# The convolution's running sum in two PSUM banks instead of the gate's SBUF tile, with another order of all instructions

## The chip, the cores and the metric

One core of a Trainium2 chip runs the whole program. The metric is the device time of one execution in microseconds (us), the median of several runs. The engines are TensorE (PE, with its weight loads shown apart as PEld), VectorE (DVE), ScalarE (ACT), GpSimd (POOL) and SyncE (SP), which issues the transfers. PSUM has eight banks of 512 numbers per partition here; PE writes its results there, and DVE and ACT read and write there too. POOL works on SBUF alone in this kernel.

## What is computed

Eight batches, eight heads, 576 positions, 64 numbers per head. Attention with a causal mask and a decay, then a gated two-layer map in which the gate is a convolution over five positions:

```
scores = q @ k.T / sqrt(64) + (cum[i] - cum[j])      # causal; cum = cumsum(log f)
x      = softmax(scores) @ v                          # (8, 576, 512)
gate   = sigmoid(sum over t of conv_w[t] * xp[:, t:t+576, :])   # xp: x with four zeros in front
out    = (gate * (x @ w_val)) @ w_out
```

## The kernel before

Work goes by pairs of heads: 32 pairs, four to a batch, so that two heads of 64 fill 128 partitions. For each pair the steps are these (the short names are the classes by which the kernel's plan knows them, and the lines are those of the kernel before):

- **TH, TL** (L374 and the helper at L260): the loaded q and k (`Xr`) are split into a high part `Xh` and a rest `Xl`; copies go to ACT, DVE or POOL, the subtraction to DVE or POOL.
- **S**: score matmuls into PSUM (L245, the helper of all matmuls).
- **sel** (L469 on DVE, L467 on POOL, L302 for the short last block): the causal mask is put into the loaded decay row `dm` or `dl`.
- **red** (L458, DVE): adds the decay, scales, and finds the row's bound `negm`; it reads PSUM and SBUF, and writes back into PSUM.
- **SX** (L462, ACT): the exponential, from PSUM to SBUF (`P`, `Pl`).
- **PT** (L503, L527, PE): transposes of the result into PSUM; **PE** (L260) copies them to SBUF (`pt`, `pl`), on ACT or DVE.
- **PV** (PE), **X** (L577, DVE): times v, times the inverse row sum, which has come back through DRAM (`rzd`); the result is `x32`, here called x.
- **xh, xl** (L260, L584): x split into two parts for the next matmul.
- **conv** (L265, L267, L619): five passes over x. The first multiplies x by one weight column into the pair's gate tile in SBUF, on ACT, DVE or POOL; the other four are scalar_tensor_tensor instructions, gate = x * weight + gate, on DVE. A POOL form was allowed for the first four pairs.
- **sig** (L590, ACT): a tanh of the gate tile in place.

After four pairs a batch's gated map follows: **Mv** (PE, x times w_val), **H** (L651, DVE, gate times that), **hh, hl** (L260, L665), **Mo** (PE, times w_out), **O** (L692, L694) and the store.

No scheduler works at run time. A table of digits, three or more for each instruction group, gives one order for the whole program: the group's number, its engine, and the PSUM banks that it takes. Every engine runs its share of this list in that order and waits on semaphores where data or a bank is not ready. A bank taken again waits for all users of what it held. `Plan.order` reads the table; the costs and priorities given to `plan.add` were for the search that made the table, and nothing reads them when the kernel is built.

Of the kernel before, what the change touches and what calls it, by code (L numbers as in the profile page):

```python
# [11 lines left out]
ALU = mybir.AluOpType  # L12
# [4 lines left out]
P = 128  # L17
D = 64
S = 576
# [9 lines left out]
NPT = 4  # L29
# [17 lines left out]
0010930z40240740430K40630q000u30a30V40C20B10D22640b30e20x30r30E20520f10d20F10s30g10h20c328001230G20i20H20I20j40J20M10P20N20Q10O22900R20S20T14040U22R42  # L47
a00X12b21442d22j0452c15b40t20-22e14242f20_12x0100Y22m22g12s062k22n12o22h22l12t00Z22p13-42z11024442y12D0421122i1340012u21212q22F22r11722v11320p052E12A0
233b21f41613722V045672w24642B13522C13925d41923811822G021a12W03a11b23c12X02H11c22Q12I42-21e33613i012K42Y22_15941d22Z13k054c35h21h13222O43023312M41k23d0
33114841i21j21l11q43x0675541m23u0023z12T41n23e03w15741p33y13l23j23v10o053f24a31o13A0160y34m0503B13o23C13p23m14b012763g13q21s13h23n34d24x034f24e10v34h2  # L50
7044g10m014i24k24j14B0214n24l10n074o25j34q24D13D061t24p14s23O013E14t24C11v23H44v23N13r23F44u14w17445i067254y27d34r11w11u23L44z17e33J45m27f14E0037245k2
5n11B45o24F17844H0475r24G13Q003s24J15l14A25p25s14K061x24I15t0354L13R27i35q14M44U25u35I0041z17g34O45v25K15E063P25f45J15x27643S11y27h001425F25z34S45w13T
34Q45A25G15C27j28b45y14V063U37l25B15D17n27m13V25L0537k15H25O0177o21A35P14X005N17q25Q14W27t37r13W27p15R067s0234Y27c35S15_13X20w35V47D008q15T43Y25M17H06
78d44_17w28r37E262054Z15Z47u27F14-25X460041D18j45028o17a47y27J18f41E20l001G27x16n079m47z28p37v17B29s47C16f006327A19q46121H17K0258h47G26415127N0439u47I
16k016527M15227O17Q057R16l05326617U46g01F27-17S45416729o46c057P16827L16d03t16926o03Z16a28s023647Y46e28t36b18n36h27W49B11I281006i18u29z16j27_058v18w29A
36p28x16m28026q18O018y38229C38z28518D0058B28A18S037ax48E28316v068F26r38T18P26w08U18H2aD48Q11J26s076x28J31M48I19E38M21K19D061238628N18K28C11L2az46t08G1
872aB4aM18Y0459w49F28L1aN38-1aF49H28Z18V0059G16u26D048X19J29K2aK31O19O0579M28W19P29I16A06cB48R29S2aP36y11X49Z009y39Q29N11R21P26E09L19-29U36z39T18_029X
29_19V29029149R1842991934a70011Q21S1a10238l4aL2a81cF49Y16B0a911T2954a31882cO1974aO01703cJ4a211U2cP29W1cH4cQ19a05cD4aQ21W3aS2aR19c02a021Z16C2aU3cR3aT1a
# [107 lines left out]
def tile_decay_attention_gated_mlp(  # L166
# [89 lines left out]
    def any_(cls, durs, prio, fn, reads=(), writes=(), **kw):  # L256
        return plan.add(cls, durs, prio, lambda e: fn(engine[e]), reads, writes, **kw)
# [566 lines left out]
```

## Time and profile before

| what | value |
|---|---|
| median of three runs | 530.08 us (527.26 to 532.85) |
| the profiled execution | 531.49 us |
| its span in the trace | 529.8 us |
| PE busy | 487.0 us (92%) |
| weight loads busy | 414.6 us (78%) |
| DVE busy | 468.6 us (88%) |
| ACT busy | 351.4 us (66%) |
| POOL busy | 159.8 us (30%) |
| mean granted TensorE clock | 0.987 |

Busy time is the time in which at least one instruction of the engine was under way. Instructions of one engine overlap a little at their ends, so the durations of single instructions add up to more than the busy time. The span is shorter than the execution's time by 1.7 us, which lie around it.

### The profile page before, as it was taken

To read this page: it belongs to the slowest core of one execution; us is meant where nothing else is said; L and a number is where in the kernel's file an instruction comes from. 1 tells how busy PE (TensorE), PEld (TensorE's weight loads), DVE (VectorE), ACT (ScalarE), POOL (GpSimd) and SP (SyncE) were. 2 spreads that over 40 slices of the span, in tenths; PEclk is the share of its full clock that TensorE was granted. 3 is DMA by queue.
4 is the path that set the end of the run, shared out by engine and by line. 5 is a ranking of instruction groups with operands and counts; after the bars stand their busy time and mean duration, and the time that the engine had idled before them with its cause. 6 is when DMAs were issued, how large, how long until landed. Compare 5 with 4: busy or idle time off the path is not lost.

```text
span 529.8 us, 13876 instructions
## 1 busy us (share of the span) xinstructions
PE 487.0 (92%) x5136; PEld 414.6 (78%) x5136; DVE 468.6 (88%) x1214; ACT 351.4 (66%) x963; POOL 159.8 (30%) x190
## 2 busy tenths in 40 slices
PE   5878989899999989999797999999999989999997
PEld 3656778777899777888696878887778878898985
DVE  6988999999998899999986998999998989989871
ACT  4978989889767664766665676777866647584020
POOL 4132625452234432222423251321312343012210
PEclk9998999899999999999998999999999999999999
DMA  6774465755555356445444437454554555521022
GB/s 205 241 247 113 124 212 151 235 159 177 157 173 172 113 170 174 131 147 173 145 128 127 147 115 251 128 163 133 144 171 142 151 141 176 180 64 37 11 81 99
DMA packets 35012, 79.57 MB, mean 150 GB/s; under 512 B 5056, under 2 KB 5312, under 8 KB 34944
## 3 DMA queue, kind: packets, MB, share of 16 engines
q1 hardware_dynamic: 34864, 78.54, 48.7%
q8 instruction: 40, 0.66, 0.5%
q14 instruction: 28, 0.23, 0.1%
q10 hardware_dynamic: 80, 0.15, 0.1%
HBM read 68.93 MB, written 9.73 MB: 148 GB/s over the span
## 4 chain that ended last, share of the span: by engine, by line
PE 44%; DVE 26%; DMA 12%; ACT 9%; issue 5%; SPq 3%; DVEq 0%; ACTq 0%
PE banks L245 38%; DVE banks L458 8%; DVE gate L619 5%; PE banks L503 4%; DMA x<-rzd 4%; DMA Xr<-in_x_dram 3%; ACT P L462 3%; SPq L271 3%; DVE dm L469 2%; ACT pt L260 2%; DMA rzd<-pl 1%; DVE negm L458 1%; PE banks L527 1%; DVE x L577 1%; ACT Pl L462 1%
## 5 line engine op out<-in xcount | busy, mean ns | idle before, releaser
L462 ACT ACTIVATE P<-banks,negm 128x128 f32<-128x128 f32 (+3 forms) x256 | 135.0, 535 | 63.8 <-DVE negm L458 60.3
L458 DVE CUSTOM_DVE_ANT_0 banks<-banks,dm 128x512 f32<-128x512 f32 (+1 forms) x240 | 115.4, 505 | 15.3 <-ACT pt L260 4.4
L619 DVE SCALAR_TENSOR_TENSOR gate<-x,cw,gate 128x576 f32<-128x576 f32 x128 | 117.6, 927 | 1.4 <-ACT gate L265 0.4
L245 PE MATMUL banks<-xh,wall 128*128 128x288 f32 x512 | 114.5, 304 | 1.2 <-DVE pt L260 0.7
L260 ACT COPY pt<-banks 128x512 f32<-128x512 f32 (+1 forms) x194 | 98.6, 538 | 24.8 <-PE banks L503 21.5
L245 PE MATMUL banks<-pt,vt 128*64 128x128 f32 (+1 forms) x1280 | 95.0, 300 | 1.3 <-DVE pt L260 0.6
L245 PE MATMUL banks<-wall,hh 128*128 128x512 f32 x288 | 91.7, 399 | 2.7 <-ACT P L462 1.6
L245 PEld LDWEIGHTS banks<-xh,wall 128*128 128x128 f32 x512 | 85.7, 189 | 5.8 <-DVE pt L260 0.9
L245 PEld LDWEIGHTS banks<-pt,vt 128*64 128x64 f32 x1280 | 76.2, 138 | 11.0 <-issue 1.8
L245 PE MATMUL banks<-xl,wall 128*128 128x288 f32 x256 | 75.9, 297 | 0.0
L503 PE MATMUL banks<-ident,P 64*128 64x64 f32 x1280 | 59.9, 230 | 16.6 <-ACT P L462 9.2
L503 PEld LDWEIGHTS banks<-ident,P 64*128 64x128 f32 x1280 | 50.2, 141 | 31.8 <-ACT P L462 15.7
L467 POOL TENSOR_SCALAR_AFFINE_SELECT dm<-dm 128x256 f32<-128x256 f32 x51 | 24.4, 481 | 126.7 <-DVE negm L458 48.5
L245 PEld LDWEIGHTS banks<-wall,hh 128*128 128x128 f32 x288 | 51.5, 188 | 13.9 <-ACT P L462 2.4
L374 POOL TENSOR_TENSOR Xl<-Xr,Xh 128x576 fp32r<-128x576 f32 (+1 forms) x30 | 46.1, 1538 | 49.9 <-ACT Xh L260 49.6
L245 PE MATMUL banks<-Xh 64*128 64x512 f32 (+2 forms) x224 | 52.9, 384 | 6.3 <-ACT Pl L462 3.5
L245 PE MATMUL banks<-wall,hl 128*128 128x512 f32 x144 | 56.3, 391 | 0.0
L462 ACT ACTIVATION_READ_ACCUMULATOR P<-banks,negm 128x1 f32 x256 | 53.2, 208 | 0.0
L245 PEld LDWEIGHTS banks<-xl,wall 128*128 128x128 f32 x256 | 48.5, 189 | 0.3
L245 PE MATMUL banks<-Xh,Xl 64*128 64x512 f32 (+2 forms) x224 | 46.6, 333 | 0.0
L245 PE MATMUL banks<-Xl,Xh 64*128 64x512 f32 (+2 forms) x224 | 46.5, 333 | 0.0
L665 POOL TENSOR_TENSOR hl<-h,hh 128x64 fp32r<-128x64 f32 (+2 forms) x22 | 23.5, 1072 | 70.1 <-DVE hh L260 38.8
(100 smaller groups left out, 761.4 us busy)
## 6 DMA issues: line engine op xcount, KB each, us to landing
Xr<-in_x_dram SPq DMA_DIRECT2D x32, 608.0 KB
dm<-decd SPq DMA_DIRECT2D x60, 256.0 KB
vt<-in_v_dram SPq DMA_DIRECT2D x32, 320.0 KB
x<-rzd SPq DMA_DIRECT2D x64, 144.0 KB
out_dram<-ot SPq DMA_DIRECT2D x36, 256.0 KB
dl<-decd SPq DMA_DIRECT2D x60, 144.0 KB
ot<-in_w_val_dram SPq DMA_DIRECT2D x2, 512.0 KB
wu<-in_w_val_dram SPq DMA_DIRECT2D x2, 512.0 KB
```

The source lines that it names most:

```text
L245: nc.tensor.matmul(out, lhsT=lhsT, rhs=rhs, start=start, stop=stop)
L260: (eng.copy if eng is nc.scalar else eng.tensor_copy)(out=out, in_=in_)
L271: lambda e: (nc.sync if e == "SP" else nc.scalar).dma_start(out=out, in_=in_), reads, writes, **kw)
L374: eng.tensor_tensor(out=Xl[r][:, a:e], in0=Xr[r][:, a:e], in1=Xh[r][:, a:e].bitcast(F32), op=ALU.subtract)
L458: nc.vector.tensor_tensor_reduce(out=sl, in0=sl, in1=add, op0=ALU.add, op1=ALU.min, scale=-0.125, scalar=3.0e38, accum_out=negm[r][:, col])
L462: nc.scalar.activation(out=dst[:, o:o + ext], in_=bank(key)[:, c0:c0 + ext], func=AF.Exp, bias=negm[r][:, col], scale=-1.0, accum_out=zs[r ...
L467: eng.affine_select(out=t, in_=t, pattern=[[0, 2], [-1, P]], base=0, channel_multiplier=1, compare_op=ALU.is_ge, fill=-BIG)
L469: eng.tensor_tensor(out=t, in0=t, in1=tri4[:, None, :].to_broadcast([P, 2, P]), op=ALU.add)
L503: nc.tensor.transpose(out=bank(key[a])[:, c:c + D], in_=Pt[ms[h]][sl, BOFF[b] + P * j:BOFF[b] + P * j + P], identity=ident[sl, sl])
L527: nc.tensor.transpose(out=t[0:m, 512 * h + D * j:512 * h + D * j + D], in_=Pl[r][sl, P * j:P * j + m], identity=ident[sl, sl])
L619: eng.scalar_tensor_tensor(out=gt, in0=src, scalar=wt_, in1=gt, op0=ALU.mult, op1=ALU.add)
L665: eng.tensor_tensor(out=hl[jj][:, y:y + x1 - x0], in0=h32[:, x0:x1], in1=hh[jj][:, y:y + x1 - x0].bitcast(F32), op=ALU.subtract)
```

## The change

The sum of the convolution gets two PSUM banks of its own, `acc`, for each pair. The first pass writes there, on DVE or ACT and no longer on POOL; the next three read and write there; the fifth pass reads the banks and writes the gate tile in SBUF. The POOL form of the later passes is gone. Some costs for the search are other numbers, and so is a group label (`mode`) of the transposes; neither reaches the program. The table is new as a whole: the order on every engine, which engine does the work that may go to several, and the banks.

```
-0010930z40240740430K40630q000u30a30V40C20B10D22640b30e20x30r30E20520f10d20F10s30g10h20c328001230G20i20H20I20j40J20M10P20N20Q10O22900R20S20T14040U22R42
+0010930240z40740b30K40s30V40r30C20B10520630a30e20E20D20F10f10G20430H20I20y30J20m000x30h20u30c30d328012340t32T40i20j40N20M12R40P20O20Q10g12900R20S20T10
...
-            pe("PT", 0.0622 * 2 * nt, p, go, [("ident",), *(("P", m, b) for m in ms for b in blocks)], key, cols=256 * nt, mode=1)
+            pe("PT", 0.0622 * 2 * nt, p, go, [("ident",), *(("P", m, b) for m in ms for b in blocks)], key, cols=256 * nt, mode=4)
...
+        acc = new(("acc", i), 2)
         for n, t in enumerate(reversed(range(KC))):
-            early = i < NPT and n > 0
-
-            def cv(eng, t=t, first=n == 0):
+
+            def cv(eng, t=t, n=n):
                 src, wt_ = xr[:, t:t + S], cw[:, t, g:g + 1]
-                if first:
-                    times(eng, gt, src, wt_)
-                elif eng is nc.gpsimd:
-                    times(eng, h32, src, wt_)
-                    eng.tensor_tensor(out=gt, in0=gt, in1=h32, op=ALU.add)
+                sums = bank(acc)[:, 0:S]
+                if n == 0:
+                    times(eng, sums, src, wt_)
                 else:
-                    eng.scalar_tensor_tensor(out=gt, in0=src, scalar=wt_, in1=gt, op0=ALU.mult, op1=ALU.add)
-            any_("conv", {"DVE": 0.76, **({"POOL": 2.2} if early else {})} if n else {"POOL": 0.73, "DVE": 0.45, "ACT": 0.67}, p + 0.1 + 0.02 * n, cv,
-                 [*xk, ("xpad", rx), ("cw",), *([gk] if n else [])], [gk, *(kh32 if early else [])])
+                    eng.scalar_tensor_tensor(out=gt if n == KC - 1 else sums, in0=src, scalar=wt_, in1=sums, op0=ALU.mult, op1=ALU.add)
+            any_("cv", {"DVE": 0.68} if n else {"DVE": 0.68, "ACT": 0.64}, p + 0.1 + 0.02 * n, cv,
+                 [*xk, ("xpad", rx), ("cw",), acc], [gk] if n == KC - 1 else [acc])
```

Lines of the changed kernel stand one to four lower than before (L619 is L615, L458 is L457, L374 is L373).

DVE, where the four later passes of the tenth pair stand (x_94 is its x, gate_110 its gate tile, dm and dl decay rows of later pairs, ISA the red instruction and the read of its result, h_112 of a gated map). In the kernel before, the first pass, one further pass, and the next one ten rows on:

```order
L267 TENSOR_SCALAR gate_110<-x_94,cw 128x576
L619 SCALAR_TENSOR_TENSOR gate_110<-x_94,cw,gate_110 128x576
L458 ISA banks,negm_90<-banks,dm_69 128x512
L458 ISA negm_90 128x1
L458 ISA banks,negm_90<-banks,dm_69 128x512
L458 ISA negm_90 128x1
L577 TENSOR_TENSOR x_95<-banks,x_95 128x192
L477 TENSOR_SCALAR Pl_83<-zs_93 128x9
L478 RECIPROCAL Pl_83<-Pl_83 128x9
L584 TENSOR_TENSOR xl_106<-x_96,xh_100 128x576
L469 TENSOR_TENSOR dm_69<-dm_69,tri_66 128x2x128
L619 SCALAR_TENSOR_TENSOR gate_110<-x_94,cw,gate_110 128x576
```

And in the changed kernel, all four passes of the same pair:

```order
L615 SCALAR_TENSOR_TENSOR banks<-x_94,cw,banks 128x576
L647 SCALAR_TENSOR_TENSOR h_112<-gate_111,banks 128x288
L615 SCALAR_TENSOR_TENSOR banks<-x_94,cw,banks 128x576 x2
L457 ISA banks,negm_91<-banks,dm_70 128x128
L457 ISA negm_91 128x1
L457 ISA banks,negm_91<-banks,dm_70 128x128
L457 ISA negm_91 128x1
L647 SCALAR_TENSOR_TENSOR h_112<-gate_111,banks 128x288
L615 SCALAR_TENSOR_TENSOR gate_110<-x_94,cw,banks 128x576
```

The passes now stand close together, since two banks are held from the first to the last of them; over all pairs DVE begins 4 to 14 groups of work from the first of them to the last, and PE 2 to 9. The second operand is a bank and no longer the gate tile, and the pair's first pass is on ACT.

POOL, from the low part of the tenth pair's x (xl_105) on; Xl_78 is the low part of q and k of the twelfth pair, Xl_77 of the thirteenth. In the kernel before:

```order
L584 TENSOR_TENSOR xl_105<-x_95,xh_99 128x576
L467 AFFINE_SELECT dm_70<-dm_70 128x2x128
L467 AFFINE_SELECT dm_69<-dm_69 128x2x128 x2
L374 TENSOR_TENSOR Xl_78<-Xr_74,Xh_76 128x640
L467 AFFINE_SELECT dm_70<-dm_70 128x2x128 x2
L374 TENSOR_TENSOR Xl_77<-Xr_73,Xh_75 128x576
```

And in the changed kernel:

```order
L583 TENSOR_TENSOR xl_105<-x_95,xh_99 128x576
L466 AFFINE_SELECT dm_69<-dm_69 128x2x128
L301 TENSOR_TENSOR dl_72<-dl_72,tri 128x64
L373 TENSOR_TENSOR Xl_78<-Xr_74,Xh_76 128x640
L373 TENSOR_TENSOR Xl_78<-Xr_74,Xh_76 128x576
```

Both halves of the twelfth pair's Xl are on POOL now, one behind the other, where DVE had the second half.

What the two tables give to each engine, where the numbers differ most:

| work | DVE before | DVE after | other engine before | after |
|---|---|---|---|---|
| conv, passes two to five | 128 | 128 | - | - |
| conv, first pass | 11 | 12 | ACT 12, POOL 9 | ACT 20, POOL 0 |
| mask of dm, 128x256 | 69 | 39 | POOL 51 | POOL 81 |
| mask of dl, 128x64 | 19 | 9 | POOL 11 | POOL 21 |
| Xl, 128x640 | 16 | 5 | POOL 12 | POOL 23 |
| xl, 128x576 | 16 | 9 | POOL 16 | POOL 23 |
| hl, 128x576 | 10 | 6 | POOL 6 | POOL 10 |
| copy of pt, 128x512 | 15 | 37 | ACT 145 | ACT 123 |

On PE the kinds and numbers of all matmuls are the same; only their order and banks differ. The transfers are the same in number and size.

## Rows read from the trace of the kernel before

**Rows 1.** Page, part 1: busy us (share of the span) and instructions of each engine

```profile
PE 487.0 (92%) x5136; PEld 414.6 (78%) x5136; DVE 468.6 (88%) x1214; ACT 351.4 (66%) x963; POOL 159.8 (30%) x190
```

**Rows 2.** Stretches: length, busy of PE, PEld, DVE, ACT, POOL, granted clock, DMA, GB/s

```profile
20.00:480.00 460.00, 428.16 (x4722) 365.70 (x4724) 421.24 (x1110) 329.06 (x919) 145.16 (x160) 0.99 0.52 156
...
0.00:20.00 20.00, 12.60 (x84) 8.21 (x84) 14.88 (x44) 12.61 (x28) 6.40 (x24) 1.00 0.74 245
...
260.00:280.00 20.00, 16.34 (x186) 15.29 (x186) 16.58 (x48) 12.93 (x39) 3.54 (x5) 0.91 0.56 166
280.00:300.00 20.00, 17.18 (x182) 15.87 (x182) 15.27 (x39) 12.20 (x35) 6.31 (x8) 0.91 0.46 134
...
500.00:520.00 20.00, 20.00 (x112) 17.68 (x111) 12.37 (x29) 3.03 (x5) 1.70 (x2) 1.00 0.16 60
```

**Rows 3.** Page, part 4: the chain that ended last, shares of the span by engine

```profile
PE 44%; DVE 26%; DMA 12%; ACT 9%; issue 5%; SPq 3%; DVEq 0%; ACTq 0%
```

**Rows 4.** All waits, longest first: who waited for whom, us, times, longest

```profile
ACT P L462 <- DVE negm L458: 60.3, 52, 3.5
...
PE banks L503 <- ACT P L462: 9.2, 8, 3.0
...
PE banks L245 <- DMA Xr<-in_x_dram: 3.0, 1, 3.0
```

**Rows 5.** DVE by form: count | busy us, mean ns | idle before, releasers

```profile
L619 DVE SCALAR_TENSOR_TENSOR gate<-x,cw,gate 128x576 f32<-128x576 f32 x128 | 117.6, 927 | 1.4 <-ACT gate L265 0.4 <-POOL gate L267 0.4
L469 DVE TENSOR_TENSOR dm<-dm,tri 128x256 f32<-128x256 f32 x69 | 34.8, 507 | 0.9
L651 DVE SCALAR_TENSOR_TENSOR h<-gate,banks 128x288 f32<-128x288 f32 x64 | 27.4, 446 | 4.9 <-PE banks L245 2.4 <-ACT gate L590 1.5
L374 DVE TENSOR_TENSOR Xl<-Xr,Xh 128x640 fp32r<-128x640 f32 x16 | 14.6, 912 | 0.2 <-ACT Xh L260 0.2
L584 DVE TENSOR_TENSOR xl<-x,xh 128x576 fp32r<-128x576 f32 x16 | 12.2, 761 | 0.1
L260 DVE COPY pt<-banks 128x512 f32<-128x512 f32 x15 | 10.1, 681 | 0.8 <-ACT pl L260 0.6 <-PE banks L503 0.2
L665 DVE TENSOR_TENSOR hl<-h,hh 128x576 fp32r<-128x576 f32 x10 | 8.7, 874 | 0.4 <-ACT hh L260 0.4
L267 DVE TENSOR_SCALAR gate<-x,cw 128x576 f32<-128x576 f32 x11 | 7.1, 641 | 0.1
L302 DVE TENSOR_TENSOR dl<-dl,tri 128x64 f32<-128x64 f32 x19 | 5.7, 297 | 0.1
```

**Rows 6.** Lines L619 and L458 (width 576): duration ns min/median/max, first and last start

```profile
L619 DVE SCALAR_TENSOR_TENSOR gate<-x,cw,gate x128: 757/812/2051, 33.9 to 512.2; 128x576 f32<-128x576 f32 x128
...
L458 DVE CUSTOM_DVE_ANT_0 banks<-banks,dl x30: 750/766/799, 45.1 to 476.6; 128x576 f32<-128x576 f32 x30
```

**Rows 7.** Chain in order of time: start us, us, what

```profile
33.87 0.83 DVE gate L619
34.72 2.05 DVE gate L619
```

**Rows 8.** Timeline of POOL at the same place: start us, us, what

```profile
34.75 1.41 POOL L584 TENSOR_TENSOR xl<-x,xh 128x576 fp32r<-128x576 f32 x1 [2.08 <-ACT xh L260]
```

**Rows 9.** ACT and POOL by form, as in rows 5

```profile
L260 ACT COPY pt<-banks 128x512 f32<-128x512 f32 x145 | 82.7, 592 | 18.5 <-PE banks L503 15.4 <-PE banks L527 2.5
L265 ACT ACTIVATE gate<-x,cw 128x576 f32<-128x576 f32 x12 | 9.4, 781 | 2.0 <-DVE x L577 2.0
...
L584 POOL TENSOR_TENSOR xl<-x,xh 128x576 fp32r<-128x576 f32 x16 | 26.4, 1648 | 20.9 <-ACT xh L260 12.6 <-DVE xh L260 8.3
L467 POOL TENSOR_SCALAR_AFFINE_SELECT dm<-dm 128x256 f32<-128x256 f32 x51 | 24.4, 481 | 126.7 <-DVE negm L458 48.5 <-DMA dm<-decd 46.7 <-DVE Pl L477 15.0
L374 POOL TENSOR_TENSOR Xl<-Xr,Xh 128x640 fp32r<-128x640 f32 x12 | 19.3, 1609 | 16.6 <-ACT Xh L260 16.4
L267 POOL TENSOR_SCALAR gate<-x,cw 128x576 f32<-128x576 f32 x9 | 8.0, 891 | 11.8 <-DVE x L577 11.7
```

More of the change, by code (lines that the diff above doesn't have):

```diff
@@ L28 @@
 NXR = 3
-NPT = 4
 R0 = 16
@@ new lines @@
+U32j0562b22d21442c10Y24642a00X12k22642q22e12o20p010-20q072l10Z22s002p12m20_12h22r12t01023-42n12f22i12D0651122g12x0722E21332F12u22A0342y1340562C22v11f4
+1222z14042w22B11722G003921613b22V042732H23522Q12I41921822K41a12W05b43723c11b23a12X02-21d12M43611c23d002O43222_11e32Y24443313i053023811q41i21h14243k063
+111k25741j21l15942Z11m23x0725d43l25543e03y13j23z11n23o143A0363f21p30n073C13p20o023g13u0764c33B13q21s14b001233m13r23w13s23v11o14d24x064f24e13h24m0454g1
+4h35j34i24B0107044a34k24j14C24n34D14q24l13D014o23O003N13E24s33H44p10v34t24v24u13F44y24w15i012344844r11t24z11u23L47f11v24E0675m23J41w13Q055k27245n11B41
@@ new lines @@
+x24F14A25l14H0261y24J25o34I14G15h35r24K010w37d35p25t0675s14L25u34U13R24O43P27g35I0455q17445x25E005v25K17843U225y15z34M41z10l057e35F25f45J13V27645G15C2
+1A35w13W27h045103t14S45A23X25D17i38f45B13n34V077l21D14Q43Y23S18b47m17j25O0635P15H27k15Q27n35R057c25L0231E25S17q25T44X045N17o25V47r11F28d47p11G27s0038h
+44W27t35M13T34Y25_17H0717w24Z17u25Z460064_247J15X47y34-37B29m45027C17D017I19q47z25127x17a48o36f077v17E28j47A162035227F19u48q27G27K0126128r36326n007L15
+326416c038t37M18p26k041H165266117Q051I26d07R17-16727S49z16g07U46829A37N0656h26l07O16e27P13Z16927W48s067356i11J27Y46a25419o46j36o01K18w29s48u28l48x1810
@@ new lines @@
+11L36m21M48v16p26q18y28S0628B27_078T18z28U16r26b18E38D0248028C18n38229y38O068F2ax49E385108H29B38316s058628J38A16t09C38P28I18M26v038Q1872aB48438N18K26w
+0aF46u28G1882aD48L19D045671O19w46x2892aM1aK3az48Y0329F29Z008-19H29G18Z29J39I18V0249-2aN39O0359K29_19M2cB48W18R26D008X29P39N1aL39L18_019S29Q2a104790199
+29T19346E09R19U2914a211R2a70219X2aP36y16A069V2cF4aJ31P29Y16B06z2a919749W11S11Q2954aO03514a81a02cD4a311T21X49a07aS2cJ4aQ2aT16C29c02aU3cO11U2aR16F21W3aX
+21V1aa059d2a40309b2ab1cQ3ak1aV2ac4aZ027a619g25ae4a-3aW1b12dM4a51a_2bc0019h2aY1b33cT3ai4b21b42b803cR3b62bd19i2ag41Z1al00b92b71cP3be19j2dU4b51dQ4ba19k2b
@@ new lines @@
+f071dO41-2bh1cS04356cH42026G1dZ21_2b01an01bg1cU2d-3211cW2am2cX1d1027cL4cY3ao26H3cV1c_2dS4bi0016I03cZ2eX4d01bj2aH4c-1bb2222bk1bl04ar10cN26N06d22232bm1b
+v1d52bn4253as2241dc04bp4d32at26J0d41d73d_3d61dd2da2e036O0de1au2bt4db1d82av2d91br4dY39l1dg047e236K2e_4e102501di19e2eZ4df2dh2dj073e52by04e32e61dl2e73dk1
+bw05e41bz2e82ea2e91dm047bx2ed36P1ec0329f3do16Q4eb1dp056L46S07fa1dz2f34dq1eg2aw1dt4ee2en05dn2bC10ei3dr4f83ej26X04f14bD2g64f93eo26Y0el2bE2dv4em1ek1gc4eh
+1bF26T0g84ep1fb2dx4ef1bG2ge46Z1er052fd2ap16-4fc01604eq26U1es2aq3et1eu037bA1fe2dC05ev1fg2bB3ff1ew2fh1dA01fi28a1dD2fl2ex036fn052ey2ez1dB2eA06fj2bI03eB1e
@@ new lines @@
+E4fk1fo3bL01gi3fr2eC4eK1fp2gl1bM0dW4ft2fm1f72f54fw2bJ0gj2dG16ga4bN2gk3bT04fq1eI4dH2fx1eG4fy00bK2i94fu2bO1gm3dI2bQ03fv1fz2bR0fs1dJ2bP3fA1ib4bU0id4dK2fC
+020i54fB2gn067156V4fE1bV2go3bS2i74fF043gp2eN00fH1gr2gq1gt2fD1gu2eL06gs1eO2bW2gv1gw2bX3fL02eM2gy070fV1fM2gx1fI061fN4gJ02gz2fK1fP4fJ1gA2fG1b_01jg4gC2ik1
+gK2gE3bY04ii3eR15jo4c00dE1eS2in3jm4ij3bH1bZ0gg4c12gL1eT2c701gB1dF3eU2c80gH2gF2c402gI1jk4b-2il3gG1eV2fR4gD1c50c21fT4gN005ji4jv1c32im06734gO1jw2gP1c62gQ
+005io2fY02gS1iq2ip1gR2is3ir1ih2fW05gM2iv2fZ2it2gT076fX2ix020iy3c92jy3ch05kr4eP2ca1gV2js3if4iu1cb2cc01iw1gU2iB2g013iz2cd0iA1g12iD3eQ3g22gW06ce1iE2g32ci
@@ new lines @@
+0jt3kt4gX1iC1iG2g-4iF1ju3h41gY4iI01iH1cj1cm00iJ2kE1kG3g42iK1h04iM056f-2kv4jx01234h24iO2cf4iN2ck4iP067jB2h505iQ2jC1iL2iR1jz2h702dL1jD3jA1f_3jG2jH1iV06j
+q4cn0iW2j31jE2kH2jF1h62jJ3jI041co1kF3h82iS065jM2lC4jX032iT1jK2iZ4jT06jY1jO2iX4jZ1cr00jP2kx4jU2jQ1hb12kJ2iU2jV1cs0hc2eW1hd2j14cw05ct1i_4he2jL1lE4jN1jR2
+hf2kI00674jS1kz4lP1jW2lR1lQ3j-013kM2hg1j402kK2j_1k01kO3kN1lS3j601kP2kR2kQ1j52kL1kD3k406j72kS1k1023kU2kT010ke2k21h91l6024k52kX2k64k31kV2ha3hk06l81cp4kW
+1ja23hh07k84l71lG4kZ2kY1hl0jb2cx0jc2kc4k-2jd2k_1hi0cy1l02hm2nK4hp01hj2lU3lI4je2hn1lT05627nG4l11ho3nI4ka4hq0lX2lK4lV2lY1hs00lZ3j81ht0l-2lW1l203hu2l_1m0
@@ L103 @@
+0Ip1DJ2Gx2Ik1Ix045HC06Iz1Gy2Gt1DN2Iy1Gz2DO3HA05HD2Iq2Iu023DR2IA06HB2Ir041IB1Iv1IE4DX05It2IK1HW4Fp1IC4Is1DS06E502HE1GA1II4HG10Ea04IG4HH2E007HF2HI2DT0Iw
+2IL03DU2Gu2HJ2IN06HK2DV2IX00IO2IM2I-01DW2IP2J306IQ2E10Jb03E21HL1I_0J607J02IY0J40IZ2J12DY0IR20J70DZ2Jc0J22D-4E34Je05J52J82Jf0J92IS2Eb0Ja2IT2E60Jd2Jg2IU
+2Jm03Jh2Jn0Ji2Jj05IV2Jk0IW1JG06E71Jl2Ec1Jo2E84Jp2Ed4Jr05Jq2Js0Jw01Jt1Ju4Jx0JB07Jy1Jz4JC0JH0JD1JE4JL01JI2JJ4JM0JN1JO4
 """
@@ L471, in plan_s @@
                     any_("sel", {"POOL": 0.36, "DVE": 0.34}, pp - (0.3 if j == 3 else 0.0), sel, [*dk2, ("tri4",)], dk2)
-                dve("red", ext / 960.0 + 0.1, pp, red, [keys[n], *dkey, *added.get(n, ())], [("red", i, u, n), ("negm", r, u, n)])
+                dve("red", ext / 960.0 + 0.075, pp, red, [keys[n], *dkey, *added.get(n, ())], [("red", i, u, n), ("negm", r, u, n)])
                 act("SX", ext / 1200.0 + 0.237, pp, ex, [keys[n], ("red", i, u, n), ("negm", r, u, n), ("act",)], [pkey, ("zs", r, u, n)])
@@ L478, in rec @@
             nc.vector.reciprocal(out=rz, in_=rz)
-        dve("rec", 0.3, base + 0.45, rec, [("zs", r, u, n) for u, group in enumerate(SG) for n in range(len(group))], [("rz", r)])
+        dve("rec", 0.33, base + 0.45, rec, [("zs", r, u, n) for u, group in enumerate(SG) for n in range(len(group))], [("rz", r)])
     def at(i, j):
@@ L527, in gol @@
                     nc.tensor.transpose(out=t[0:m, 512 * h + D * j:512 * h + D * j + D], in_=Pl[r][sl, P * j:P * j + m], identity=ident[sl, sl])
[L528 removed]
+        pe("PT", 0.31, p, gol, [("ident",), ("Pl", r), ("rz", r)], [key], cols=640, mode=4)
         def two(m, a, e):
```

85 lines of the change are left out of this document (28 added, 57 removed).

## The prediction

> **What bounds the kernel now.** I read the busy times first. PE is busy 487.0 us of 529.8 and DVE 468.6 [rows 1]: two engines near full, ACT and POOL far from it. Next the stretches, to part the ends of the program from its middle. In the first 20 us PE does 12.6 us of work, because it waits for the first scores, and towards the end it is busy without a gap (20.00 of 20) while DVE falls off [rows 2]. Between 20 and 480 us PE is busy 428.2 of 460 us and DVE 421.2: idle 31.8 and 38.8. So in the middle both engines are over 91% full, and neither is alone the bound. Two engines that feed each other at such shares cannot both be full: scores wait for DVE's red, the exponential on ACT waits for it, and the transposes on PE wait for the exponential. The list of waits shows this: ACT's exponential waits 60.3 us in all for DVE's negm, and PE in turn waits 9.2 us at the transposes for ACT's P [rows 4]. The chain that ended last has 44% PE, 26% DVE, 12% transfers and 9% ACT [rows 3]. DVE's 26% of 529.8 us are 137.7 us in which nothing but DVE's work moved the end.
>
> [...]
>
> **The passes of the convolution.** In SBUF the 128 passes take 927 ns on average [rows 5], but 757 at least and 812 in the median, with 2051 at the worst [rows 6]. The mean is far above the median, so something lengthens some of them. The worst one shows what: it begins at 34.72 [rows 7], POOL begins an xl subtraction of 1.41 us at 34.75 [rows 8], and the pass lasts 2.05 us; the pass before it, with no such partner, lasts 0.83. So 128 x (927 - 757) = 21.8 us of DVE's time look like waiting for POOL.
>
> No row shows the new form. The nearest is DVE's red of the same width: it reads PSUM and SBUF, writes PSUM, and takes 750 to 799 ns, 766 in the median [rows 6]. It is also never long, though POOL works beside it at times. H, which reads PSUM and SBUF and writes SBUF, takes 446 for half the width [rows 5]. I take 766 for each new pass, the median of the row that matches in width, operands and target. Saved: 128 x (927 - 766) = 20.6 us of DVE. The bounds: nothing, if the long passes have another cause than POOL and the new ones keep a mean of 927; and 21.8, if they cost 757.
>
> [...]
>
> The first pass goes from 11 to 12 on DVE, at 641 ns before [rows 5]; with PSUM as target I bound it by 641 and 766 and take 1 us more in all (0.6 to 2.1). ACT gets 8 more at 781, +6.2 us, and POOL loses 9 at 891, -8.0 us [rows 9].
>
> **The work that moves.** By the two tables and the rows' means, DVE loses 30 masks of dm (x 507 = 15.2), 11 Xl of 640 (x 912 = 10.0), 7 xl (x 761 = 5.3), 10 masks of dl (x 297 = 3.0) and 4 hl (x 874 = 3.5), and gains 22 copies of pt (x 681 = 15.0) [rows 5]. Net 22.0 us less. The other kinds change by a few each, in both directions, and I take them as nothing. ACT loses the 22 copies at 592, 13.0 us [rows 9]; with the first passes it ends near 345. POOL gains 30 x 481 + 11 x 1609 + 7 x 1648, 43.6 us, less the 8.0 of first passes [rows 9], and comes to 195 us, and some 10 more with the masks of dl and the hl that it takes over, 39% of the span. POOL's cover is its idle time of 370 us [rows 1]; where the Xl of a pair is late there, its scores wait on PE.
>
> **The sum.** DVE: -20.6 + 1.0 - 22.0 = -41.6 us, from 468.6 to 427. PE's matmuls are the same in kind and number, so its work is unchanged, and so are the transfers. How much reaches the end? If the chain keeps its shape and DVE's 137.7 us of it shrink as DVE's work does, by 41.6 / 468.6 = 8.9%, the end comes 12.2 us earlier. If DVE never held PE up any more, at most PE's idle 31.8 us of the middle could go. Less than 12.2, down to nothing, comes out if the saved time only makes DVE wait for PE. I take 12.2: in the middle DVE is as full as PE, so its relief should count, but the last 50 us and the first 20 are PE's and gain nothing. From the profiled execution, 531.5 - 12.2 = 519.3; that execution lay 1.4 us above the median shown, so the median to expect is 518.
>
> What the banks cost: a pair now holds two of eight banks from its first pass to its fourth read, at least 4 x 0.766 = 3.1 us, and by the order 4 to 14 DVE groups, say up to 8 us. Over 32 pairs this is 196 to 512 bank-us of 8 x 529.8 = 4238, 5 to 12%. Behind a pass that waits for its banks stand the next pair's red instructions, and behind those ACT and PE. In the likeliest case I cost this at nothing, because the passes are closed up in the new order; if it were not covered, each 0.4 us of added PE wait per pair would cost the whole gain (32 x 0.38 = 12.2).
>
> **The rivals.**
> - *DVE's relief is real and PE's gaps go too.* With DVE at 427 us its idle time in the middle about doubles, and PE's 31.8 us could shrink by four fifths: 531.5 - 25 - 1.4 = 505. For it: the waits at ACT for DVE are the longest of all [rows 4]. Against: part of PE's gaps have other ends, such as 3.0 us for one transfer of Xr.
> - *PE binds, and DVE's slack is spent on waiting.* PE is 93% full in the middle already. Then only a third of 12.2 us comes through: 526. For it: half of PE's gaps may follow from the order of dependent work, not from DVE's load. A late POOL gives the same number: 11 more Xl there take 1609 instead of 912 ns, 7.7 us more if each lies on PE's path [rows 5, 9], which takes 12.2 down to 4.5.
> - *Banks: slower than before.* If each pair's two banks make PE wait one pass longer (0.766 us) at a bank, 32 x 0.766 = 24.5 us are lost against 12.2 gained: 531.5 + 12.3 - 1.4 = 542. It decides from 0.38 us per pair on, and costs over 1% of the time from 0.55 us on. For it: transposes and scores take banks in turn, and PE often takes one just freed. Against: the passes stand close together, and DVE frees its other banks sooner.
> - *PSUM passes are no shorter than 927 ns.* The term of 20.6 falls away, DVE loses 21 us, and 6.2 of the 12.2 us remain: 524. [...] Against: the red of the same width.
>
> **How the numbers follow.** The forecast, 512 to 523: 0.45. The fuller gain, 500 to 512: 0.18. PE binds or POOL is late, 523 to 532: 0.22. PSUM passes cost as before, about 524: 0.03. Banks, 532 to 545: 0.12. About 1% is what a measurement of this kernel tells from no change, so 5.3 us: faster is below 524.8, slower above 535.4. Faster takes the first two, the fourth, and a little of the third: 0.71. Slower takes most of the banks' case: 0.09. The rest, 0.20, is the same. The range leaves out the far ends of the fuller gain and most of the banks' case: 504 to 532. The likeliest case's own range is 512 to 523.
>
> **What would show each step.** The passes, L615: a median of 766, and above all no long tail; a mean over 850 makes the term wrong. DVE busy near 427 and ACT near 345 and POOL near 205 us: right if within 10. In the middle, PE's idle time should fall from 31.8 to about 20 us; if it stays while DVE's grows, PE's own order binds. ACT's waits for DVE's negm should fall from 60.3 us. If PE's longest waits come to be for the passes at L615, the banks' rival is right; if for Xl on POOL, the late POOL. The forecast is wrong if DVE falls to 427 and the time does not fall by 5 us.

## The result and the profile after

The changed kernel takes 497.26 us in the median (496.64 to 497.92, four runs) against 528.67 of the kernel before beside it: a ratio of 0.940, with a 95% interval of 0.933 to 0.947. It is 31.4 us faster, and lies below the lower end of the forecast's range, 504. The profiled execution took 497.07 us, its span 495.4.

First the page's busy times and the chain by engine, and from the view of cores the span with the mean granted clock:

```profile
PE 477.6 (96%) x5136; PEld 413.2 (83%) x5136; DVE 425.5 (86%) x1172; ACT 347.7 (70%) x943; POOL 197.3 (40%) x252
...
PE 66%; DVE 10%; issue 10%; DMA 7%; POOL 4%; ACT 2%; SPq 1%; POOLq 0%; DVEq 0%; ACTq 0%
...
core 0: 495.4 us, clock 0.999
```

Against [rows 1, 3] DVE's busy time fell by 43.1 us, POOL's rose by 37.5, and the chain that ended last is now PE's: 66% where it was 44%, with DVE at 10% after 26%. PE's own busy time fell too, from 487.0 to 477.6 us, though it runs the same matmuls.

The stretch from 20 to 480 us (length; busy time of PE, PEld, DVE, ACT, POOL with counts; granted clock, DMA share, GB/s):

```profile
20.00:480.00 460.00, 453.15 (x4979) 394.92 (x4976) 410.10 (x1128) 332.08 (x908) 187.48 (x223) 1.00 0.54 159
```

PE's idle time in it is 6.9 us, against 31.8 in [rows 2]. DVE is 89% busy there, nearly as full as before, because its work passes in less time. Over the whole span, PE's idle time went from 42.8 to 17.8 us. These 25.0 us and the 9.4 of PE's busy time are the 34.4 us by which the span is shorter.

The passes, DVE and the longest waits. First the duration of the passes (ns min/median/max, first and last start) and who waited for them, then DVE, ACT, POOL and PE by form (count | busy us, mean ns | idle before), then waits (us in total, times, longest):

```profile
L615 DVE SCALAR_TENSOR_TENSOR banks<-x,cw,banks x96: 808/819/824, 30.6 to 474.7; 128x576 f32<-128x576 f32 x96
L615 DVE SCALAR_TENSOR_TENSOR gate<-x,cw,banks x32: 801/809/815, 33.2 to 476.6; 128x576 f32<-128x576 f32 x32
...
  PEld banks L244: 0.6, 2
  PEld banks L502: 0.4, 1
```

```profile
L615 DVE SCALAR_TENSOR_TENSOR banks<-x,cw,banks 128x576 f32<-128x576 f32 x96 | 78.6, 819 | 4.9 <-ACT banks L264 3.7
...
L615 DVE SCALAR_TENSOR_TENSOR gate<-x,cw,banks 128x576 f32<-128x576 f32 x32 | 25.9, 810 | 0.4
...
L468 DVE TENSOR_TENSOR dm<-dm,tri 128x256 f32<-128x256 f32 x39 | 19.0, 489 | 0.3
...
L266 DVE TENSOR_SCALAR banks<-x,cw 128x576 f32<-128x576 f32 x12 | 9.8, 817 | 0.4 <-ACT pt L259 0.4
...
L264 ACT ACTIVATE banks<-x,cw 128x576 f32<-128x576 f32 x20 | 15.0, 748 | 2.3 <-ACT pl L259 0.7 <-ACT P L461 0.5 <-ACT pt L259 0.4
...
L373 POOL TENSOR_TENSOR Xl<-Xr,Xh 128x640 fp32r<-128x640 f32 x23 | 36.9, 1603 | 21.2 <-ACT Xh L259 13.7 <-issue 3.7 <-PE banks L244 2.0
...
L502 PE MATMUL banks<-ident,P 64*128 64x64 f32 x1280 | 61.0, 228 | 3.3 <-ACT P L461 1.9 <-ACT Pl L461 0.5 <-DVE pt L259 0.4
```

```profile
POOL dm L466 <- DVE negm L457: 123.5, 43, 11.8
ACT P L461 <- DVE negm L457: 33.5, 41, 2.8
...
PE banks L502 <- ACT P L461: 1.9, 5, 0.6
```

No pass lasts over 824 ns; in [rows 6] the worst lasted 2051. PE's weight loads wait 1.0 us in all for the passes. ACT's wait for negm went from 60.3 to 33.5 us and PE's at the transposes from 9.2 to 1.9 [rows 4].

### The profile page after: what moved, and what is told of

It is laid out like the page before. It is cut to its first block, busy times and chain, and to the rows that moved or that the text cites. A ratio compares the mean times of both kernels' runs of the same rounds, so it can differ in the third digit from the quotient of the medians.

```text
span 495.4 us, 13912 instructions
## 1 busy us (share of the span) xinstructions
PE 477.6 (96%) x5136; PEld 413.2 (83%) x5136; DVE 425.5 (86%) x1172; ACT 347.7 (70%) x943; POOL 197.3 (40%) x252
## 4 chain that ended last, share of the span: by engine, by line
PE 66%; DVE 10%; issue 10%; DMA 7%; POOL 4%; ACT 2%; SPq 1%; POOLq 0%; DVEq 0%; ACTq 0%
PE banks L244 58%; PE banks L502 6%; DVE banks L457 3%; DMA x<-rzd 2%; PE banks L526 2%; DMA dm<-decd 2%; DMA dl<-decd 2%; DVE banks L615 1%; POOL Xl L373 1%; ACT P L461 1%; POOL dm L466 1%; POOL wall L741 1%; DVE negm L457 1%; DVE pt L259 1%; DMA h<-in_conv_w_dram 1%
## 5 line engine op out<-in xcount | busy, mean ns | idle before, releaser
L461 ACT ACTIVATE P<-banks,negm 128x256 f32<-128x256 f32 (+3 forms) x256 | 134.3, 530 | 34.8 <-DVE negm L457 33.5
L457 DVE CUSTOM_DVE_ANT_0 banks<-banks,dm 128x512 f32<-128x512 f32 (+1 forms) x240 | 115.2, 506 | 13.6 <-POOL dm L466 5.0
L244 PE MATMUL banks<-xh,wall 128*128 128x288 f32 x512 | 111.6, 300 | 0.2 <-ACT Pl L461 0.2
L259 ACT COPY pt<-banks 128x512 f32<-128x512 f32 (+1 forms) x168 | 85.2, 532 | 29.4 <-PE banks L502 27.6
L466 POOL TENSOR_SCALAR_AFFINE_SELECT dm<-dm 128x256 f32<-128x256 f32 x81 | 34.9, 434 | 153.9 <-DVE negm L457 123.5
L615 DVE SCALAR_TENSOR_TENSOR banks<-x,cw,banks 128x576 f32<-128x576 f32 x96 | 78.6, 819 | 4.9 <-ACT banks L264 3.7
L373 POOL TENSOR_TENSOR Xl<-Xr,Xh 128x640 fp32r<-128x640 f32 (+1 forms) x43 | 65.2, 1521 | 25.6 <-ACT Xh L259 16.0
L244 PE MATMUL banks<-Xh 64*128 64x512 f32 (+3 forms) x224 | 53.2, 376 | 1.8 <-ACT pt L259 0.6
L244 PE MATMUL banks<-Xh,Xl 64*128 64x512 f32 (+3 forms) x224 | 47.0, 328 | 0.0
L244 PE MATMUL banks<-Xl,Xh 64*128 64x512 f32 (+3 forms) x224 | 46.3, 325 | 0.0
L457 DVE DVE_READ_ACCUMULATOR2_ANT negm<- 128x1 f32 x288 | 40.5, 141 | 0.0
```

The source lines that it names most:

```text
L244: nc.tensor.matmul(out, lhsT=lhsT, rhs=rhs, start=start, stop=stop)
L259: (eng.copy if eng is nc.scalar else eng.tensor_copy)(out=out, in_=in_)
L373: eng.tensor_tensor(out=Xl[r][:, a:e], in0=Xr[r][:, a:e], in1=Xh[r][:, a:e].bitcast(F32), op=ALU.subtract)
L457: nc.vector.tensor_tensor_reduce(out=sl, in0=sl, in1=add, op0=ALU.add, op1=ALU.min, scale=-0.125, scalar=3.0e38, accum_out=negm[r][:, col])
L461: nc.scalar.activation(out=dst[:, o:o + ext], in_=bank(key)[:, c0:c0 + ext], func=AF.Exp, bias=negm[r][:, col], scale=-1.0, accum_out=zs[r ...
L466: eng.affine_select(out=t, in_=t, pattern=[[0, 2], [-1, P]], base=0, channel_multiplier=1, compare_op=ALU.is_ge, fill=-BIG)
```

## The experiments

The kernel before lay between 526 and 529 us beside each group of runs. The ratios are to it, with their intervals. Times are medians; the executions of one run lie up to about 6 us apart (e5, e13). DVE, the passes and the PE gaps are from the one profiled execution of each run; the gaps are 460 us less PE's busy time between 20 and 480 us. "Reads off" means that POOL's subtractions are memsets.

| run | order | sum | DVE us | mean of a pass ns | PE gaps us | time us | ratio |
|---|---|---|---|---|---|---|---|
| before | old | SBUF | 468.6 | 927 | 31.8 | 528.7 | 1 |
| changed | new | PSUM | 425.5 | 817 | 6.9 | 497.3 | 0.940 [0.933, 0.947] |
| e1 | new | SBUF | 462.6 | 1105 | 32.2 | 534.4 | 1.015 [1.011, 1.020] |
| e2, old engines | new | PSUM | 455.4 | 815 | 34.9 | 541.1 | 1.025 [1.019, 1.031] |
| e3, old engines | new | SBUF | 471.4 | 936 | 41.3 | 555.4 | 1.055 [1.049, 1.062] |
| e4, new engines | old | SBUF | 456.5 | 930 | 45.8 | 551.3 | 1.045 [1.041, 1.050] |
| e5, reads off | old | SBUF | 443.6 | 829 | 16.9 | 509.8 | 0.965 [0.958, 0.972] |
| e6, load | new | PSUM | 456.8 | 817 | 22.9 | 524.4 | 0.995 [0.992, 0.997] |
| e7, narrow | old | SBUF | 426.8 | 562 | 21.8 | 516.7 | 0.978 [0.972, 0.985] |
| e8, reads off | new | SBUF | 424.5 | 838 | 14.4 | 506.2 | 0.960 [0.954, 0.965] |
| e9, reads off, load | old | SBUF | 467.1 | 817 | 25.4 | 522.0 | 0.990 [0.986, 0.993] |
| e10, irregular load | new | PSUM | 439.4 | 817 | 13.0 | 507.4 | 0.962 [0.957, 0.967] |
| e11, steady load | new | PSUM | 437.6 | 817 | 10.2 | 506.0 | 0.959 [0.955, 0.963] |
| e12, narrow | new | PSUM | 397.1 | 486 | 6.4 | 494.3 | 0.937 [0.933, 0.941] |
| e13, reads off, narrow | old | SBUF | 404.0 | 494 | 12.9 | 504.5 | 0.956 [0.949, 0.963] |
| e14, reads off | new | PSUM | 422.3 | 817 | 7.1 | 498.6 | 0.946 [0.939, 0.952] |
| e15, load | old | SBUF | 496.8 | 888 | 44.6 | 549.6 | 1.043 [1.036, 1.050] |

### One part undone, or alone: e1 to e4

e1, the sum back in SBUF (pair 6 alone keeps its banks):

```diff
-                sums = bank(acc)[:, 0:S]
+                sums = bank(acc)[:, 0:S] if i == 6 else gt
```

> The changed kernel with one part undone: the sum stands in the gate's SBUF tile again (pair 6 alone keeps its banks, because its tile is still in use for weights), in the new order, with the new engines and without any use of the banks that the table sets aside. The passes' mean should go from 817 ns back to about 927 or more, since POOL is busier now: 128 x 0.11 = 14 us more of DVE, some 440 us. Theory 'load' (time follows DVE's busy time; 31 us came from 43 us less): 497 + 0.73 x 14 = 507 us. Theory 'order' (the new order of dependent work brought the gain, and DVE's load only a little): 497 to 501 us. Theory 'lock' (passes of up to 2 us behind POOL's subtractions held up the red instructions behind them): 512 us or more.

Measured: 534.4 us, 37 us more than the changed kernel and slower than the kernel before. The passes are much longer than I expected. POOL's subtractions are longer too (1763 ns for an Xl of 640, 1603 in the changed kernel). DVE and the passes, then POOL, by form:

```profile
L615 DVE SCALAR_TENSOR_TENSOR gate<-x,cw,gate 128x576 f32<-128x576 f32 x124 | 137.0, 1105 | 5.3 <-ACT gate L264 3.8
...
L373 POOL TENSOR_TENSOR Xl<-Xr,Xh 128x640 fp32r<-128x640 f32 x23 | 40.5, 1763 | 24.2 <-ACT Xh L259 16.5 <-issue 2.8 <-DVE Xh L259 2.7
```

So theory "order" falls: with the sum in SBUF beside POOL's reads, nothing is left of the new order's gain. The other two theories are not parted here, since DVE's busy time rose by 37.1 us and not by the 14 expected.

e2, e3 and e4 set the engine digits of the table and leave the positions. In e2 and e3 the new table has the old engines (e3 with e1's line as well); in e4 the old table has the new ones. In the new table 102 groups of masks stand on POOL and 48 on DVE, with the old engines 62 and 88; of the copies of a bank 186 stand on ACT and 70 on DVE, with the old engines 218 and 38. The first line of e2's table, in which only digits change:

```diff
-0010930240z40740b30K40s30V40r30C20B10520630a30e20E20D20F10f10G20430H20I20y30J20m000x30h20u30c30d328012340t32T40i20j40N20M12R40P20O20Q10g12900R20S20T10
+0010930240z40740b30K40s30V40r30C20B10520630a30e20E20D20F10f10G20430H20I20y30J20m000x30h20u30c30d228012340t22T40i20j40N20M12R40P20O20Q10g12900R20S20T10U2
```

> The changed kernel, its order and its banks, with all work that may go to several engines (masks, splits, copies of pt, but not the convolution) on the engine that it had in the kernel before. DVE gets the 22 us back that had moved, about 448 us, and POOL falls to some 155 us. Load: 497 + 0.73 x 22 = 513 us. Order: up to 503 us. Lock: near 500 us, since the passes stay in PSUM.

> The order of the changed kernel alone: the sum in SBUF as in e1 and the old engines as in e2. DVE about 462 us, 6 us below the kernel before. Load: 497 + 0.73 x 37 = 524 us. Order: 505 us or less. Lock: 512 us or more.

> The kernel before, its order and its sum in SBUF, with the engines of the changed kernel for all work that may go to several, first passes included. DVE falls by about 20 us to 448 us, POOL rises to some 205 us. Load: 529 - 0.73 x 20 = 514 us. Order: 525 us or more. Lock: 527 us or more, for POOL's subtractions meet the passes more often.

Measured: 541.1, 555.4 and 551.3 us, all slower than the kernel before, though DVE is busy 13 and 12 us less in e2 and e4. No theory had this. An order is made together with its engines: a group that stands at a place where POOL would have had time may come late or early on DVE, and the groups behind it would wait. That is argued and not followed in the traces. These three therefore do not price the moved work.

### POOL's reads: e5, e8, e14

On POOL the subtractions for Xl, xl and hl take one column, and memsets of about the same length stand for the others; on DVE they stay.

```diff
-                eng.tensor_tensor(out=Xl[r][:, a:e], in0=Xr[r][:, a:e], in1=Xh[r][:, a:e].bitcast(F32), op=ALU.subtract)
+                rest(eng, Xl[r][:, a:e], Xr[r][:, a:e], Xh[r][:, a:e].bitcast(F32))
...
+    def rest(eng, out, in0, in1):
...
+        eng.tensor_tensor(out=out[:, 0:1], in0=in0[:, 0:1], in1=in1[:, 0:1], op=ALU.subtract)
+        n = out.shape[-1]
+        for m in ((n, n, n // 4) if n > 64 else (n,)):
+            eng.memset(out[:, n - m:].bitcast(F32), 0.0)
```

> The kernel before, with the three kinds of subtraction on POOL (Xl, xl, hl) replaced by one column of the subtraction and memsets of about the same length: POOL is as long busy, waits for the same inputs, but reads almost nothing (these rests are zero then, on POOL only). If the long passes come from POOL's reads, their mean falls from 927 to under 800 ns and DVE from 469 to about 448 us. Theory 'lock' (such waits, which no order can plan, are what held the kernel): 505 to 512 us. Theory 'fit' (an order is made for certain durations and engines, and gains only with a new table): 520 us or more. Theory 'load' (0.73 us of time for each us of DVE, as first seen): 511 us.

> e1 (new order, sum in SBUF) with POOL's subtractions replaced as in e5. If e1's 37 us come from the passes and POOL's reads holding each other up, the passes fall from 1105 to under 830 ns and the time to 497 to 503 us. If the place of the sum matters by itself (waits by bank or by tile), it stays above 515 us.

> The changed kernel, sum in PSUM, with POOL's subtractions replaced as in e5 and e8: what e8 has beside the place of the sum. If e8's 9 us above the changed kernel come from the memsets being longer on POOL than the subtractions (1.53 against 1.43 us and 1.8 against 1.6): 503 to 507 us here too. If they come from the sum's place: 495 to 499 us.

Measured: e5 509.8 us, with the passes at 829 ns (814 in the median). That lies in the range of theory "lock" and next to the 511 of "load", so e5 does not part them. e8 506.2 us, between its two cases, with the passes at 838 instead of 1105 and DVE at 424.5: of the 37 us that e1 had added, 28 are gone by that alone. e14 498.6 us, within 0.3% of the changed kernel. The passes of e1 and of e8 (min/median/max):

```profile
L615 DVE SCALAR_TENSOR_TENSOR gate<-x,cw,gate x124: 803/838/2011, 31.6 to 516.8; 128x576 f32<-128x576 f32 x124
```

```profile
L625 DVE SCALAR_TENSOR_TENSOR gate<-x,cw,gate x124: 805/816/1653, 30.7 to 487.5; 128x576 f32<-128x576 f32 x124
```

So the long passes come with POOL's reads, in either order: with these off, the mean goes from 927 to 829 ns (e5) and from 1105 to 838 (e8). With the sum in PSUM and the reads on, the longest pass of the changed kernel lasts 824 ns. (A memset is also another kind of instruction than a subtraction. That reading is what matters is borne out by casts, which read too: in the kernel before, three passes of 1217 to 1267 ns stand beside casts alone, and in e5's trace one of 1266 ns; no pass there is long beside a memset alone.) e8's last 9 us are not the memsets' length, since e14 has the same memsets. In e8 some passes are still long, with a mean of 838 ns over a median of 816: POOL goes on reading for other work, and the longest pass, 1653 ns, stands beside an instruction of 1437 that makes weights (`wall`). And PE waits 4.2 us for Xl, against 0.6 in e14. Which of the two costs more was not tried.

### How much DVE's time is worth: e6, e7, e9 to e13, e15

More work on DVE (e6: 160 columns behind 96 passes; e9 and e15: 64 columns of the gate tile behind every later pass; e10: 576 columns behind 19 passes drawn at random; e11: 62 columns behind 64), or less (e7 and e13: 256 of 576 columns in four passes; e12: in three):

```diff
                     eng.scalar_tensor_tensor(out=gt if n == KC - 1 else sums, in0=src, scalar=wt_, in1=sums, op0=ALU.mult, op1=ALU.add)
+                    if n < KC - 1:
+                        eng.tensor_scalar(out=sums[:, 0:160], in0=sums[:, 0:160], scalar1=1.0, scalar2=None, op0=ALU.mult)
...
-                    eng.scalar_tensor_tensor(out=gt, in0=src, scalar=wt_, in1=gt, op0=ALU.mult, op1=ALU.add)
+                    eng.scalar_tensor_tensor(out=gt[:, 0:256], in0=src[:, 0:256], scalar=wt_, in1=gt[:, 0:256], op0=ALU.mult, op1=ALU.add)
```

> The changed kernel with an added multiplication by 1.0 of 160 columns in PSUM behind each pass but the last on DVE (128 less those on ACT and the fifth: 96 of 128 passes, and the 12 first passes on DVE), about 0.38 us each: 37 to 41 us of DVE, as much as e1 added, but the same each time and with nothing shared with POOL. Load and fit: as in e1, 530 to 538 us. Lock: clearly less than e1, 505 to 518 us, since a steady load is absorbed in DVE's idle time of 50 us in the middle.

> The kernel before with passes two to five cut to 256 of 576 columns (the gate is wrong beyond them): each is 0.33 us shorter, 43 us less of DVE in all, as much as the change took off. Load: 526 - 31 = 495 us. Fit: 515 us or more, the rest of the gain being the new order's. Lock: between, about 510 us, since the passes can still be held by POOL.

> e5 (old order, POOL's reads off, 510 us) with a multiplication by 1.0 of 64 columns of the gate tile behind each later pass on DVE, about 0.2 us each and 25 us in all: DVE is back at about 469 us, as in the kernel before, but with no pass held. Theory 'load' (the amount of DVE work decides): about 526 us, as the kernel before. Theory 'irregular' (passes held for up to 1.2 us at places that no order knows cost more than their sum spread evenly): 518 us or less.

> The changed kernel with a multiplication by 1.0 of 576 columns in PSUM behind 19 passes out of 96, drawn at random: 19 x 0.77 = 14.6 us of DVE, about the sum and the number of the passes that POOL held in the kernel before. Load: 497 + 0.87 x 14.6 = 510 us, as e11. Irregular: at least 5 us more than e11.

> The changed kernel with a multiplication by 1.0 of 62 columns behind the second and the fourth pass of every pair: 64 x 0.23 = 14.7 us of DVE, the same sum as e10, evenly spread. Load: 510 us. Irregular: 500 to 505 us, taken by DVE's idle time in the middle.

> The changed kernel with passes two to four cut to 256 of 576 columns (the gate is wrong beyond them): 96 x 0.33 = 32 us less of DVE. If PE binds now (its gaps in the middle are 7 us): 490 to 496 us. If DVE still binds (0.87 us for each us, as in e6): 470 to 478 us, which PE's 478 us of work do not allow, so 485 us at the least.

> e5 and e7 together: the old order with POOL's reads off and passes two to five cut to 256 columns (the gate is wrong beyond them): DVE about 402 us, no pass held. If the old order can use any relief of DVE once POOL holds nothing: 490 to 500 us, near the changed kernel. If the old order has a floor of its own that DVE does not set: 503 to 510 us, near e5. e7's 517 us with the reads on stand beside it: the difference is what held passes cost where DVE has time to spare.

> The kernel before with the small multiplication of e9 behind each later pass: 25 to 31 us more of DVE, POOL's reads on. If the slope that e9 shows (12 us for 24 us) holds at this point too: 538 to 542 us. If the old order is at its knee here, as the new one is at its own: 548 us or more. If the small operations in SBUF wait for POOL themselves, their mean is over 0.24 us and the time higher by that.

Measured, as slopes (us of time for each us of DVE's busy time, differences of the table):

- Old order, reads on: e15 to before 20.9 / 28.2 = 0.74; before to e7 12.0 / 41.8 = 0.29.
- Old order, reads off: e9 to e5 12.2 / 23.5 = 0.52; e5 to e13 5.3 / 39.6 = 0.13.
- New order: e6 to changed 27.1 / 31.3 = 0.87; e10 and e11 to changed 10.1 / 13.9 and 8.7 / 12.1, 0.73 and 0.72; changed to e12 3.0 / 28.4 = 0.11.

A us of DVE cost 0.11 to 0.29 us below some load, and 0.52 to 0.87 us above it. This knee is not the same everywhere. In the new order the slope turns near the changed kernel's 425 us. In the old order it turns somewhere between the runs at 404 and 467 us with the reads off, and between 427 and 497 us with them on; three points each don't place it closer, and the 5.3 us behind the 0.13 are within the scatter of e5's and e13's executions. The lowest that the old order came to is 500 to 507 us (the runs of e13), the new one 494, where PE is 97% busy (page of e12):

```profile
PE 475.6 (97%) x5136; PEld 412.3 (84%) x5136; DVE 397.1 (81%) x1172; ACT 346.8 (70%) x943; POOL 197.5 (40%) x252
```

Theory "irregular" does not show in e10 against e11: 1.4 us apart at nearly the same sum, where 5 were expected. Theory "lock", as I put it for e6 (a steady load is absorbed), is wrong as well: e6 cost 27 us, though less than the 33 or more of "load" and "fit", with 31.3 us on DVE where 37 to 41 were planned (the added operation took 332 ns, not 380). Not all of that is the price of DVE's time, since the added work also keeps the banks longer. Who waited for the passes in e6, us and times (nothing on PE itself in the changed kernel):

```profile
  PE banks L244: 4.1, 7
...
  PE banks L502: 1.9, 3
```

Of the other expectations, e7 met theory "fit", e12 "PE binds", and e13 the floor. e9's 522.0 fell between its two cases. e10 and e11 came out 3 to 4 us below "load". e15 met its second case, with some of the third: its small operations took 265 ns against 240 in e9, 128 x 25 ns = 3.2 us.

But holds cost something beyond DVE's busy time in the old order: the kernel before is 6.7 us above e9 (4.5 by the runs beside e9) with DVE alike (468.6 and 467.1), and e7 lies about 9 us above the line from e5 to e13 at its 427 us of DVE (509.8 - 0.13 x 16.8 = 507.6). Part of it may be POOL's side of the hold: POOL's means are 1648 ns for xl, 1491 for an Xl of 576 and 1522 for an hl of 576 in the kernel before, and 1433, 1427 and 1430 in the changed one. The runs don't part the two.

## Why the prediction was wrong

**The forecast of DVE's work held, by terms that did not.** DVE came to 425.5 us where 427 was forecast; ACT 347.7 (345), POOL 197.3 (205). The passes were mis-sized twice. I took 757 ns, the shortest row, for a pass that nothing holds; only three of the 128 are that short, each right behind a reciprocal. The runs show 812 (median of the kernel before), 816 in e8 and 819 in PSUM: 3 to 7 ns part the places, and the held time was 128 x (927 - 812) = 14.7 us, not 21.8. The red instruction at 766 was the wrong neighbour for the new form; the median of the old form was the right one. The passes saved 117.6 - 78.6 - 25.9 = 13.1 us of busy time instead of 20.6. The first pass into PSUM cost 817 on DVE, above my bound of 766, 2.7 us more in all instead of 1. Two things made up for both. The kinds that I had listed as moving gave 24.1 us of busy time instead of 22.0, the masks alone 15.8 (34.8 to 19.0). And some 8.6 us came off kinds that I had taken as nothing, such as the addition of a small number to the row sums at L477, from 9.7 to 6.5. That the forecast of the sum held is thus partly luck.

**The step that failed is how much reaches the end.** I scaled the 137.7 us that DVE has in the chain by 8.9% and took 12.2 us. A share of a chain is an average over all its places; it gives no slope. My 12.2 / 41.6 is 0.29, and the slopes measured run from 0.11 to 0.87. The number 0.29 does come out in e7: 41.8 us off DVE, in the old order and with the reads on POOL left, gave 12.0 us. But the change did more than take work off DVE, and for that my sum had no term. It counted the end of the holds as 20.6 us of DVE's time like any other, and the new order and a shorter busy time of PE as nothing. By the runs the 31.4 us divide about so: the end of the holds in the old order 18.9 (before to e5; 17.3 by the runs beside e5) for only 25.0 us of DVE, the rest of DVE's relief down to 425 us 2.3 (0.13 x 18.1), and 10.2 for the new order with its engines and the sum in PSUM (to 497.3).

The 10.2 are not the order's by itself. e8 has the new order and engines at 424.5 us of DVE, with the reads off and the sum in SBUF, and takes 506.2 us: 1.3 below the 507.5 of the old order's line. The other 8.9 come with the sum's place, which also ends the holds that e8 still has (up to 1653 ns there, 824 in the changed kernel). No run has the sum in PSUM in the old order, whose table sets no banks aside for it, so what PSUM would give without a new order stays open. And the new order gains only at low load: at 457 us of DVE it takes 524.4 (e6), and the old one, reads off, about 517 on the line from e5 to e9.

**The range was too short by a term that the sum did not have.** The range's lower end rests on the rival that lets 25 of PE's 31.8 us of gaps go, and 24.9 of them went. PE's busy time I held fixed. It fell by 9.4 us, and with it unchanged the time would have been about 507, inside the range. The clock explains only a part: the mean granted clock rose from 0.987 to 0.999, and 0.012 of 487.0 us are 5.8 us, an estimate from these numbers. e6 shows that busy time grows without the clock: 488.6 us at a granted clock of 0.997. Its transposes take 228 ns in the mean, as in the changed kernel, but fill 62.6 us and not 61.0, so they overlap less:

```profile
L502 PE MATMUL banks<-ident,P 64*128 64x64 f32 x1280 | 62.6, 228 | 8.7 <-ACT P L461 4.5 <-DVE gate L615 1.9 <-DVE pt L259 1.1
```

Over all runs a longer busy time goes with longer gaps: 475 to 484 us where the gaps are under 20 us, 483 to 500 where they are over 20. So in these runs gaps on PE went with a loss beyond their length.

**The rivals.** "PE's gaps go too" came nearest, at 505 us, with a chance of 0.18; PE's busy time was missing from it, and 497 lies below its own 500 to 512. "PE binds" is true of the changed kernel, after the gain and not instead of it. The late POOL did not come: weight loads wait 0.7 us in all for Xl and the matmuls not at all, and POOL itself waits 123.5 us for DVE's negm. The banks' rival fell, with 1.0 us of waits for the passes. The fourth rival, passes that cost as much in PSUM as before, fell too: the mean is 817 ns against 927, and the medians are 819 and 809 in PSUM against 812 in SBUF. The first pass on DVE went from 516 to 817 ns in the median when its target moved to PSUM.

The old form's row for that, of the kernel before (min/median/max):

```profile
L267 DVE TENSOR_SCALAR gate<-x,cw x11: 458/516/1678, 33.3 to 481.8; 128x576 f32<-128x576 f32 x11
```

**The pass behind it.** That POOL holds the passes was read from one place [rows 7, 8]. It is so throughout: in the trace before, 17 of the 128 passes last over 900 ns (1116 to 2051), and beside every one POOL runs an instruction that reads SBUF, a subtraction, a cast or a first pass. e5, e8 and e14 show the cause by taking reads away. In the changed kernel POOL runs something beside 84 of the 128 passes, and the longest of all lasts 824 ns.

## What to carry to other kernels

A share of the critical chain is no slope. Here, with two engines near 90% busy, a us taken off DVE was worth 0.52 to 0.87 us above a knee and 0.11 to 0.29 below it, so the gain is better bounded by the other engine's gaps (PE's, of which 25.0 us went), plus what its own busy time gives back when they close (here 9.4 us). A DVE pass with two SBUF operands beside a POOL that reads is worth a try with one operand in PSUM, if two banks can be had: here the medians were 819 and 809 ns there and 812 in SBUF, and the longest pass lasted 824 against 2051. An order searched for certain engines and places is to be changed as a whole; its parts alone (e1 to e4) were all slower than either kernel.

## What the runs showed that was not expected

- The holds came with longer instructions on both sides: in e1 the passes went from 817 to 1105 ns in the mean and POOL's Xl of 640 from 1603 to 1763.
- A pass over 576 columns costs the same in PSUM (809 to 819 ns in the median) as in SBUF (812 to 816), while the first pass, a tensor_scalar over as many columns, took 0.30 us more with PSUM as its target (516 to 817). ACT's first pass is a little shorter there, 748 against 781 ns [rows 9].
- PE's busy time is not fixed by its matmuls: the same 5136 took 475 to 500 us in these runs, and the granted clock, 0.97 to 1.00, explains only a part (e6: 488.6 us at 0.997).
